# An own tile for the last step of a weight conversion, and other places for three steps of an attention pipeline among seven block products

## The chip, the cores and the metric

The kernel runs on one core of one Trainium2 chip. The metric is the device time of one execution in microseconds (us). A core has a tensor engine (PE), a vector engine (DVE), a scalar engine (ACT), GpSimd (POOL) and SyncE (SP), which issues nearly all transfers here. Each engine takes its instructions in the order of its own stream.

## The reference, cut to what matters

Attention without a mask whose softmax is taken over the features for q and over the sequence for k, then two feed-forward layers. The arrays of q, k and v are 8 x 8 x 576 x 64 in float32; the four weights are 512 x 2048 and 2048 x 512 in float64.

```python
q_s = softmax(q, axis=-1)                  # over the 64 features
k_s = softmax(k, axis=2)                   # over the 576 positions
kv  = einsum('bhsd,bhse->bhde', k_s, v)
x   = einsum('bhsd,bhde->bhse', q_s, kv)   # then 4608 tokens x 512
h = x @ w_in;  g = h / (1 + exp(-1.702 * h));  x = g @ w_out      # first layer
h = x @ w_in2; g = maximum(0.01 * h, h);       return g @ w_out2  # second layer
```

## The kernel before, in words

The 4608 tokens are nine chunks of 512, one for each batch entry and a rest. A float32 operand is held as two halves of a reduced format (hi and lo), and a product of two operands is three matmuls: hi·hi, lo·hi, hi·lo. The first matrix of a layer is applied to two chunks at a time, in blocks: seven products (ha, hb, hc in the names, six matmuls each) in place of eight, with sums of operands made beforehand and sums of results made on VectorE. One such group is a quad (`quad_step`); a pair of chunks has eight. The order of the products in a quad is a11, s2, s1, a12, s3, s4, and after a stretch of second-layer matmuls (acc) a22. Between the products stand numbered gaps, 0 to 9, lists of other work that is recorded there: gap 0 is ahead of the first product, gap 1 behind it, gap 2 behind the second, gap 4 behind the fourth. Pairs of layer 0 are named by their first chunk: (0,2) means layer 0, chunks 2 and 3. Eight quads serve the first matrix of the pair (`pair_first`) and the second matrix of its first chunk; then come sixteen steps for the second matrix of its second chunk (`pair_second`), called (0,3) for the pair (0,2).

While a pair is worked on, the attention of the next pair's chunks runs beside it, in units of one batch entry and two heads. `Units.tick()` starts a unit each quad and holds three at a time, in stages that it puts into the gaps:

- unit a: q and k are read. `k1` (L433) is the maximum of k over the rows of each partition, kmx.
- unit b: `k2` (L452) transposes kmx on TensorE into kma; `k3` (L457) reduces it to km on VectorE; `k4` (L462) transposes km back, spread over partitions, as kmb; `k5` (L468) subtracts it from the k tile kt, `k5b` (L476) takes the exponential on ScalarE. `q2` to `q4` are the same for q (qtp, L552). `k6` (L483) multiplies k and v to kvp; `k7` divides by the sums (krs, L495, L496) and writes the halves of kvt for two heads, L505 on ScalarE and L506 on VectorE in turn. Then `next_load` issues the loads for a unit to come, into the tiles that this unit has just freed.
- unit c: the x product (L591) multiplies q with kvt into pxt, and a ScalarE copy (L622) takes it to xr.

From pair (0,2) on, kma, kmb, qtp, kvp and pxt share one bank of PSUM, so each waits until the one before it has been read.

The weights of the second layer come as float64 and are converted in 32 steps while layer 0 runs, from (0,3) on (`conv_step`). `d0` loads a raw block (L94 or L100, raw). `d1` reads its low words (L110) and its high words (L113) on ScalarE into the two halves of a tile cv. `d2` works on them on VectorE: L117, L118, L127, and the last addition L131. `d3` stores the result (o<-cv, L210, or w<-cv, L213). The raw tile and cv come from one group of two buffers with the tag c4.

A framework with tiles sets the final order on each engine, the waits and the reuse of buffers when the program is built. The order in which the source records the instructions is where it starts from; it may move an instruction ahead of others that do not depend on it, unless `keep_in_program_order` holds it, as it does L110.

The code below is the kernel before, with the line numbers of the profile. In the changed kernel the lines behind 892 stand two lower.

Of the kernel before, what the change touches and what calls it, by code (L numbers as in the profile page):

```python
# [8 lines left out]
F32 = mybir.dt.float32  # L9
F32R = mybir.dt.float32r  # L10
AF = mybir.ActivationFunctionType
ALU = mybir.AluOpType
AX = mybir.AxisListType
U32 = mybir.dt.uint32
# [12 lines left out]
def tile_softmax_linear_attention_two_mlps(  # L27
# [16 lines left out]
    nc = tc.nc  # L44
    B, H, S, D = q.shape
    NT, DM = out.shape
    DFF = w_in1.shape[1]
    P = 128
    T = 512
# [31 lines left out]
    pool = dict(sb=sb, xa=xa)  # L81
# [22 lines left out]
    def words(raw):  # L104
        t = raw.bitcast(U32).rearrange("p (n two) -> p n two", two=2)
        return t[:, :, 0], t[:, :, 1]
# [8 lines left out]
    def convert2(w):  # L115
        wf = w.bitcast(F32)
        nc.vector.tensor_scalar(out=wf, in0=wf, scalar1=F64_LOW, scalar2=F64_HIGH, op0=ALU.max, op1=ALU.min)  # L117
        nc.vector.tensor_scalar(  # L118
            out=w, in0=w, scalar1=3, scalar2=0x3FFFFFF8, op0=ALU.logical_shift_left, op1=ALU.bitwise_and
        )  # L120

    def convert3(raws, low, w):
        n = 0
        for raw in raws:
            hw = words(raw)[1]
            o = slice(n, n + T)
            nc.vector.scalar_tensor_tensor(  # L127
                out=w[:, o], in0=hw, scalar=0xC0000000, in1=w[:, o], op0=ALU.bitwise_and, op1=ALU.bitwise_or
            )
            n += T  # L130
        nc.vector.tensor_tensor(out=w, in0=w, in1=low, op=ALU.add)  # L131

    WI = {}
    WO = {}
# [53 lines left out]
    part = {}  # L188
# [11 lines left out]
    def d2(n):  # L200
        r, t = part[n]
        convert2(t[:, 1, :])
        convert3([r], t[:, 0, :], t[:, 1, :])
        part[n] = t

    def d3(n):
        w = part.pop(n)[:, 1, :].bitcast(F32)
        f, i = divmod(n, 2)
        if i:
            nc.sync.dma_start(out=o32d[f // 2][:, f % 2, :], in_=w)  # L210
            return
        for b in range(2):
            nc.sync.dma_start(out=w4d[1][f // 2][:, BLOCK[f % 2, b], :], in_=w[:, 2 * P * b : 2 * P * (b + 1)])  # L213
# [251 lines left out]
    def k5(b, j):  # L465
        mv = kst.pop((b, j))[:, 0:P].rearrange("p (h d) -> p h d", h=2)
        km, *rest = kin[b, j]
        nc.vector.tensor_tensor(  # L468
            out=km, in0=km, in1=mv[:, :, None, :].to_broadcast([P, 2, km.shape[2], D]), op=ALU.subtract
        )  # L470
        for kr in rest:
            nc.vector.tensor_tensor(out=kr, in0=kr, in1=mv, op=ALU.subtract)

    def k5b(b, j):
        for t in kin[b, j]:
            nc.scalar.activation(t, t, AF.Exp)  # L476

    def k6(b, j):
        (km, *rest), (vm, vr) = kin.pop((b, j)), vin.pop((b, j))
        pk = bank("kvp", "h")  # L480
        for r in range(R + 1):
            for h in range(2):
                nc.tensor.matmul(  # L483
                    pk[h * D : (h + 1) * D, 0 : D + 1],
                    rest[0][:, h, :] if r == R and rest else km[:, h, r, :],
                    vm[:, h, r, :] if r < R else vr[:, h, :],
                    start=(r == 0),
                    stop=(r == R),
                )
        kst[b, j] = pk  # L490
# [283 lines left out]
    def new_g(side, f):  # L774
        if split:
            if f % 2 == 0:
                whole["g"] = pool["g"].tile([P, 2, T], F32, tag="a11", name="gs", bufs=4)
            return whole["g"][:, f % 2, :]
        if side == 1:
            return sb.tile([P, T], F32, tag="gf", name="gf", bufs=3)  # L780
        gb[f] = pool["gb"].tile([P, T], F32, tag="gb", name="gb", bufs=NF)
        return gb[f]
# [76 lines left out]
    def units_of(chunks):  # L859
        return [(c, j) for c in chunks for j in range(NP)]  # L860
# [12 lines left out]
    def empty():  # L873
        return [[] for _ in range(GAPS)]

    class Units:

        def __init__(self, chunks, done):  # L880
            self.todo = units_of(chunks)
            self.pipe = [None, None]
            self.done = done

        def tick(self):
            a = self.todo.pop(0) if self.todo else None
            b, c = self.pipe
            self.pipe = [a, b]
            out = empty()

            def at(i, fn, *u):
                out[i].append(lambda: fn(*u))

            if c:
                at(0, x_product, *c)
                at(0, self.done, *c)
            if b:
                at(1, q1b, *b, (1,))
                if b[0] < B:
                    at(2, k2, *b)  # L900
                    at(2, k3, *b)
                at(4, q2, *b)
                if b[0] < B:
                    at(4, k4, *b)
                    at(4, k5, *b)
                    at(5, k5b, *b)
                at(6, q3, *b)
                at(6, q4, *b)
                if b[0] < B:
                    at(8, k6, *b)  # L910
                    at(8, k7, *b)
                at(9, next_load)
            if a:
                at(8, q1, *a)
                if a[0] < B:
                    at(8, k1, *a)
                at(9, q1b, *a, (0,))
            return out
# [269 lines left out]
    def give(*names):  # L1188
        for name in names:
            pool[name].release()  # L1190
# [14 lines left out]
        k5=lambda j: k5(0, j), ke=lambda j: k5b(0, j), k6=lambda j: k6(0, j), k7=lambda j: k7(0, j),  # L1205
# [18 lines left out]
    units = Units([2, 3], x_raw)  # L1224
# [4 lines left out]
    for s in range(NF + LATER):  # L1229
        if own.busy:  # L1230
            gaps = own.tick()
        elif s % 2 == 0:
            half = units.tick() if units.busy and s + 1 < NF + LATER else empty()
            gaps = half[:5] + empty()[5:]
        else:
            gaps = empty()[:5] + half[5:]
# [9 lines left out]
        if s < NF:  # L1246
            h = g1(1, s)
            t = new_g(1, s)
# [32 lines left out]
        if s >= LATER:  # L1281
            h = g1(2, s - LATER)
            t = new_g(2, s - LATER)
# [121 lines left out]
    def chunks_of(layer, c):  # L1405
        return [c, c + 1] if c < LAST else [c]
# [41 lines left out]
    for i, (layer, c) in enumerate(order):  # L1448
        nxt = order[i + 1] if i + 1 < len(order) else None
        if split and c < LAST:  # L1450
            work = work_of(layer, c, nxt)
            fetched.clear()
            for n in range(NQ):
                gaps = empty()
                work(n, gaps)
                quad_apart(layer, n, gaps)
            pair_apart(c, second_steps(None, nxt), fetched)
        elif c < LAST:
            units = Units(chunks_of(*nxt), x_raw) if layer == 0 else None
            pair_first(layer, c, units, held, work_of(layer, c, nxt))  # L1460
            steps = second_steps(units, nxt)
            if layer == 0:
                for f in (0, 3, 6, 9, 11, 13):
                    spread(steps, conv_step(), f)
            else:
                spread(steps, sum_pieces(range(SUMS, NQ)), 0)
            held = pair_second(layer, c + 1, steps)
            if layer == 1:
                tail(*held)
                held = None  # L1470
                give("gb")
                sb.release()
                give("cv", "lo")
                take("left", "lo", "cv")
                take("right", "g")
                split = True
        elif layer == 0:
            assert not conv_step()
            sum_steps = sum_pieces(range(SUMS))
            places[:] = [1] * 4 + [0] * 6 + [1] * 4  # L1480
            pieces = build_pair(0)
            quad_pieces = first_quad(1, 0)[:1] + [lambda: None] + first_quad(1, 0)[1:]

            def work(f):
                if f + 3 < NF:
                    load_wi(layer, f + 3)
                load_wo(layer, f)
                if f == 0:
                    load_blocks(0)
                elif sum_steps:  # L1490
                    sum_steps.pop(0)()
                if f == 0:
                    load_x2(0)
                    load_x2(1)
                if 3 <= f < 12:
                    run(pieces[f - 3])
                if f >= 10:
                    quad_pieces.pop(0)()
                    if f >= 13:
                        quad_pieces.pop(0)()  # L1500
                if f >= 14:
                    load_o32(f - 14)

            held = single(layer, c, held, work)
            run(quad_pieces)
            for items in pieces[9:]:
                run(items)
        else:
            def work(f):
                if f + 3 < NF:  # L1510
                    load_wi(1, f + 3)
                load_wo(1, f)

            tail(*single(layer, c, None, work))
# [31 lines left out]
```

## Time and profile before

| | us |
|---|---|
| median of three runs | 1624.74 |
| the three runs | 1630.39, 1624.74, 1620.43 |
| the profiled execution | 1626.16 |
| its span, from the first instruction to the last | 1624.2 |
| TensorE busy in it | 1580.5 |
| mean granted clock of TensorE | 0.998 of full speed |

The profile comes from one execution. Busy time of TensorE is modelled: matmuls overlap, and a step of 512 columns takes 0.227 us where nothing waits. A row of the timeline says when an instruction starts, how long it takes, its engine, line, operation and operands, and in brackets how long its engine stood idle just before it and what ended that. A row of waits says who waited for whom, the sum in us, how often, and the longest. A landing time is counted from the issue of a transfer.

### The profile page before, as it was taken

The page shows a single profiled execution, that of the slowest core. Times are in us where ns is not written, and L with a number is a line of the kernel's source. Part 1 is how long each engine was busy: PE and PEld are TensorE (multiplying, and loading weights), DVE is VectorE, ACT ScalarE, POOL GpSimd, SP SyncE. Part 2 cuts the span into 40 slices and gives each one's busy share as a digit, 9 for nine tenths or more (in the row PEclk, how much of TensorE's full clock was granted, in tenths as well). Part 3 has the DMA queues.
Part 4 walks back from the last instruction along what each step waited for, and adds up shares of the span by engine and source line. Part 5 has one row for each costly group of instructions (what it writes and reads, how often), then busy time and mean ns, then how long its engine had stood idle before and what let it go on. Part 6 is the DMA issues. An engine that isn't in the chain of part 4 may idle for free.

```text
span 1624.2 us, 22216 instructions
## 1 busy us (share of the span) xinstructions
PE 1580.5 (97%) x7588; PEld 1275.0 (78%) x7588; DVE 1081.6 (67%) x1703; ACT 811.3 (50%) x1734; POOL 33.3 (2%) x167
## 2 busy tenths in 40 slices
PE   5999999999999999999999999999999999999998
PEld 3677777888777788788788888888888888888887
DVE  7899769887777767767544666644774486547411
ACT  7787755566545655435333545333453354334422
POOL 1000000000000000000000000000000000000000
PEclk9999999999999999999999999999999999999999
DMA  7788577888788887978996877986776777676763
GB/s 210 229 280 254 167 237 247 267 257 261 257 284 253 252 273 238 310 261 279 314 320 230 320 275 262 321 283 208 240 210 203 235 211 213 196 229 194 223 193 102
DMA packets 221904, 397.84 MB, mean 245 GB/s; under 512 B 57696, under 2 KB 138592, under 8 KB 221792
## 3 DMA queue, kind: packets, MB, share of 16 engines
q1 hardware_dynamic: 221792, 396.43, 76.2%
q8 instruction: 60, 0.98, 0.3%
q14 instruction: 52, 0.43, 0.1%
HBM read 306.18 MB, written 90.18 MB: 244 GB/s over the span
## 4 chain that ended last, share of the span: by engine, by line
PE 75%; DMA 6%; DVE 4%; issue 3%; ACT 2%; SPq 1%; POOL 0%; ACTq 0%; DVEq 0%; POOLq 0%
PE acc L824 22%; PE hb L767 12%; PE ha L767 8%; PE hc L767 8%; PE h L754 7%; PE ob L1091 6%; PE oa L1091 4%; PE oc L1091 4%; DMA o<-cv 2%; DMA w<-cv 2%; PE pxt L591 1%; PE otp L1039 1%; DMA qt<-in_q_dram 1%; DVE gl L87 1%; ACT cv L113 1%
## 5 line engine op out<-in xcount | busy, mean ns | idle before, releaser
L824 PE MATMUL acc<-gh,wo 128*128 128x512 f32 x1152 | 363.3, 396 | 2.9 <-ACT wo L84 1.8
L824 PEld LDWEIGHTS acc<-gh,wo 128*128 128x128 f32 x1152 | 211.3, 188 | 49.6 <-ACT wo L84 2.2
L824 PE MATMUL acc<-gl,wo 128*128 128x512 f32 x576 | 225.5, 392 | 0.0
L754 PE MATMUL h<-x,wi 128*128 128x512 f32 x768 | 190.5, 397 | 2.8 <-ACT wi L84 2.8
L754 PEld LDWEIGHTS h<-x,wi 128*128 128x128 f32 x768 | 143.5, 190 | 36.7 <-ACT wi L84 4.4
L767 PE MATMUL ha<-x,wa 128*128 128x512 f32 x624 | 162.3, 391 | 3.2 <-ACT p L940 2.7
L767 PEld LDWEIGHTS ha<-x,wa 128*128 128x128 f32 x624 | 115.8, 188 | 28.4 <-ACT p L940 3.9
L87 DVE TENSOR_TENSOR sl<-a,sh 128x1024 fp32r<-128x1024 f32 x84 | 102.7, 1223 | 49.3 <-ACT sh L84 49.0
L84 ACT CAST sh<-a 128x1024 fp32r<-128x1024 f32 x84 | 88.2, 1051 | 94.4 <-PE oc L1091 35.1
L824 PEld LDWEIGHTS acc<-gl,wo 128*128 128x128 f32 x576 | 108.1, 188 | 24.3 <-issue 0.6
L991 DVE TENSOR_TENSOR a<-hb,a 128x512 f32<-128x512 f32 x72 | 49.7, 691 | 92.8 <-PE hb L767 91.5
L767 PE MATMUL hb<-x,wc 128*128 128x512 f32 x384 | 97.4, 389 | 0.0
L528 ACT ACTIVATE qt<-qt,qmx 128x64 f32<-128x64 f32 x256 | 86.1, 339 | 13.2 <-DVE qmx L518 7.8
L1091 PE MATMUL ob<-sh,wo 128*128 128x512 f32 x288 | 91.6, 394 | 0.0
L767 PE MATMUL hb<-xb,wb 128*128 128x512 f32 x336 | 86.1, 390 | 0.0
L767 PEld LDWEIGHTS hb<-x,wc 128*128 128x128 f32 x384 | 72.1, 188 | 15.0
L84 ACT CAST gh<-gf 128x512 fp32r<-128x512 f32 x96 | 59.1, 616 | 43.7 <-DVE gf L792 37.1
L87 DVE TENSOR_TENSOR gl<-gb,gh 128x512 fp32r<-128x512 f32 x80 | 54.7, 687 | 39.0 <-ACT gh L84 38.7
L824 PE MATMUL acc<-wo,gh 128*128 128x512 f32 x256 | 78.9, 390 | 0.4 <-DMA wo<-wp 0.4
L84 ACT CAST gh<-gb 128x512 fp32r<-128x512 f32 x80 | 49.0, 618 | 57.6 <-PE acc L824 57.2
L87 DVE TENSOR_TENSOR gl<-gf,gh 128x512 fp32r<-128x512 f32 x96 | 66.0, 687 | 17.6 <-ACT gh L84 16.5
L788 ACT ACTIVATE a<-a 128x512 f32<-128x512 f32 x72 | 45.5, 632 | 64.2 <-DVE a L991 64.2
(191 smaller groups left out, 2899.3 us busy)
## 6 DMA issues: line engine op xcount, KB each, us to landing
wo<-wo SPq DMA_DIRECT2D x144, 512.0 KB, 4.7
wo<-wp SPq DMA_DIRECT2D x68, 512.0 KB, 3.6
wo<-wt SPq DMA_DIRECT2D x48, 512.0 KB, 3.6
wa<-wq SPq DMA_DIRECT2D x40, 512.0 KB, 4.4
wb<-wq SPq DMA_DIRECT2D x40, 512.0 KB, 4.5
wc<-wq SPq DMA_DIRECT2D x40, 512.0 KB, 4.7
raw<-in_moe_w_in_dram SPq DMA_DIRECT2D x32, 512.0 KB, 5.2
raw<-in_moe_w_out_dram SPq DMA_DIRECT2D x32, 512.0 KB, 4.9
```

The lines of the kernel that those rows point to most:

```text
L84: nc.scalar.copy(hi, src)
L87: nc.vector.tensor_tensor(out=lo, in0=src, in1=hi.bitcast(F32), op=ALU.subtract)
L113: nc.scalar.activation(w.bitcast(F32), hw.bitcast(F32), AF.Abs)
L528: nc.scalar.activation(t[:, h, r, :], t[:, h, r, :], AF.Exp, bias=mx[:, h, r : r + 1], accum_out=sm[:, h, r : r + 1],)
L591: nc.tensor.matmul(pv[:, :, a:e], w, m[:, :, a:e], start=(i == 0), stop=(i == 2))
L754: nc.tensor.matmul(h, WI[f][:, b, wh, o * P : (o + 1) * P], xs[f"a{side}{b + 1}"][xh][:, o, :], start=(i == 0), stop=(i == n - 1),)
L767: nc.tensor.matmul(h, w[:, wh, o * P : (o + 1) * P], xo[xh][:, o, :], start=(start and i == 0), stop=(i == 5), skip_group_check=not start,)
L788: nc.scalar.activation(t, h, AF.Prelu, alpha=0.01)
L824: nc.tensor.matmul(acc[d], lhsT, rhs, start=(f == 0 and i == 0), stop=(f == NF - 1 and i == 2))
L991: add = lambda out, h, t: nc.vector.tensor_tensor(out=out, in0=h, in1=t, op=ALU.add)
L1039: nc.tensor.transpose(pt[:, r * P : (r + 1) * P], t[:, r * P : (r + 1) * P], ident)
L1091: nc.tensor.matmul(banks[name][d], w[:, l, wh, sl], x[:, l, :], start=first_one, stop=(m == NQ // 2 - 1 and l == 1 and i == 2), skip_group ...
```

## The change

The change has two parts.

The conversion's addition L131 no longer writes into cv. It writes a tile of its own, co, with one buffer, and the store reads co. The tile cv is free when L131 has read it.

`Units` takes three numbers: the gap of the x product when the tick has a unit b, the gap of k2 and k3, and the gap of k4 and k5 (the exponential stands one gap behind). By default they are 0, 2 and 4 as before, but k2 to k5b are now recorded ahead of q1b and q2 of the same gap. The units that run beside pairs of layer 0 get 4, 1 and 2.

```diff
-    def convert3(raws, low, w):
+    def convert3(raws, low, w, to=None):
...
-        nc.vector.tensor_tensor(out=w, in0=w, in1=low, op=ALU.add)
+        nc.vector.tensor_tensor(out=w if to is None else to, in0=w, in1=low, op=ALU.add)
...
     def d2(n):
         r, t = part[n]
         convert2(t[:, 1, :])
-        convert3([r], t[:, 0, :], t[:, 1, :])
-        part[n] = t
+        part[n] = pool["cv"].tile([P, T], U32, tag="co", name="co", bufs=1)
+        convert3([r], t[:, 0, :], t[:, 1, :], part[n])
 
     def d3(n):
-        w = part.pop(n)[:, 1, :].bitcast(F32)
+        w = part.pop(n).bitcast(F32)
...
-        def __init__(self, chunks, done):
+        def __init__(self, chunks, done, gaps=(0, 2, 4)):
+            self.gaps = gaps
...
+            xg, mg, sg = self.gaps
             if c:
-                at(0, x_product, *c)
-                at(0, self.done, *c)
+                at(xg if b else 0, x_product, *c)
+                at(xg if b else 0, self.done, *c)
             if b:
+                if b[0] < B:
+                    at(mg, k2, *b)
+                    at(mg, k3, *b)
                 at(1, q1b, *b, (1,))
                 if b[0] < B:
-                    at(2, k2, *b)
-                    at(2, k3, *b)
+                    at(sg, k4, *b)
+                    at(sg, k5, *b)
+                    at(sg + 1, k5b, *b)
                 at(4, q2, *b)
-                if b[0] < B:
-                    at(4, k4, *b)
-                    at(4, k5, *b)
-                    at(5, k5b, *b)
...
-            units = Units(chunks_of(*nxt), x_raw) if layer == 0 else None
+            units = Units(chunks_of(*nxt), x_raw, (4, 1, 2)) if layer == 0 else None
```

Three places show what the built programs make of it. The first is TensorE in one quad of pair (0,4), from the end of the second-layer matmuls of the quad before. Before:

```order
L824 MATMUL acc_5001<-gl,wo 128x512
L767 MATMUL ha<-x,wa 128x512 x4
L591 MATMUL pxt<-qTh,kvt_142 128x4x96 x2
L591 MATMUL pxt<-qTl,kvt_142 128x4x96
L591 MATMUL pxt<-qTh,kvt_146 128x4x32 x2
L591 MATMUL pxt<-qTl,kvt_146 128x4x32
L767 MATMUL ha<-x,wa 128x512 x2
L767 MATMUL hb<-xb,wb 128x512 x6
L452 MATMUL kma<-ident,kmx 128x128
L767 MATMUL hc<-x,wb 128x512 x6
L767 MATMUL ha<-x,wa 128x512 x6
L462 MATMUL kmb<-ident,km 128x128
```

Changed:

```order
L824 MATMUL acc_5007<-gl,wo 128x512
L767 MATMUL ha<-x,wa 128x512 x6
L452 MATMUL kma<-ident,kmx 128x128
L767 MATMUL hb<-xb,wb 128x512 x6
L462 MATMUL kmb<-ident,km 128x128
L767 MATMUL hc<-x,wb 128x512 x6
L767 MATMUL ha<-x,wa 128x512 x6
L591 MATMUL pxt<-qTh,kvt_142 128x4x96 x2
L591 MATMUL pxt<-qTl,kvt_142 128x4x96
L591 MATMUL pxt<-qTh,kvt_146 128x4x32 x2
L591 MATMUL pxt<-qTl,kvt_146 128x4x32
```

The x product (pxt) stood inside the first product and stands behind the fourth; kma came up by one product, kmb by two, and one product now lies between them.

The second is VectorE in the same pair, from the end of one quad into the next (p, u and v are sums of products, krs and kvt belong to unit b of the quad that ends, kmx to the unit whose k tile is being loaded, km to the next quad's unit b). Before:

```order
L506 SCALAR_TENSOR_TENSOR kvt_142<-kvp,krs,kvt_142 64x64
L131 ISA cv_5432<-cv_5432 128x1024
L433 TENSOR_REDUCE kmx<-kt 128x128
L538 RECIPROCAL qsm<-qsm 128x8
L935 TENSOR_TENSOR u_5415<-hb,p_5399 128x512
L457 TENSOR_REDUCE km<-kma 128x1
L935 TENSOR_TENSOR v_5430<-hc,p_5399 128x512
L468 TENSOR_TENSOR kt<-kt,kmb 128x640
```

Changed:

```order
L506 SCALAR_TENSOR_TENSOR kvt_142<-kvp,krs,kvt_142 64x64 x2
L433 TENSOR_REDUCE kmx<-kt 128x128
L457 TENSOR_REDUCE km<-kma 128x1
L538 RECIPROCAL qsm<-qsm 128x8
L937 TENSOR_TENSOR u_5419<-hb,p_5399 128x512
L468 TENSOR_TENSOR kt<-kt,kmb 128x640
L937 TENSOR_TENSOR v_5433<-hc,p_5399 128x512
L131 ISA co<-cv_5436 128x1024
```

km moved from behind u to directly behind kmx, the subtract L468 ahead of v, and the conversion's addition L131 from ahead of kmx to behind v.

The third is ScalarE near the end of (0,3), where a unit's kvt is made. Before, then changed, in one piece each:

```order
L110 ACTIVATE cv_4538<-raw_4480 128x512
L84 CAST gh<-gb 128x512
L505 ACTIVATE kvt_145<-kvp,krs 64x64 x2
L622 COPY xr<-pxt 128x512
L84 CAST gh<-gb 128x512
L84 CAST x<-xr 128x1024
```

```order
L110 ACTIVATE cv_4538<-raw_4475 128x512
L84 CAST gh<-gb 128x512
L505 ACTIVATE kvt_145<-kvp,krs 64x64
L113 ACTIVATE cv_4653<-raw_4606 128x512
L505 ACTIVATE kvt_145<-kvp,krs 64x64
L84 CAST gh<-gb 128x512
L622 COPY xr<-pxt 128x512
```

L113 of the next conversion step, which reads a raw block, now stands between the two halves of kvt.

## Rows read from the trace of the kernel before

**Rows 1.** The page: busy time of engines; shares of the chain that ended last.

```profile
PE 1580.5 (97%) x7588; PEld 1275.0 (78%) x7588; DVE 1081.6 (67%) x1703; ACT 811.3 (50%) x1734; POOL 33.3 (2%) x167
PE 75%; DMA 6%; DVE 4%; issue 3%; ACT 2%; SPq 1%; POOL 0%; ACTq 0%; DVEq 0%; POOLq 0%
```

**Rows 2.** Stages: us, then busy us by engine, clock, DMA share, GB/s.

```profile
255.00:390.00 135.00, 134.32 (x737) 109.07 (x736) 118.75 (x219) 86.47 (x233) 5.61 (x35) 1.00 0.78 255
...
461.00:575.00 114.00, 108.62 (x596) 86.58 (x595) 86.88 (x165) 64.60 (x185) 5.05 (x30) 1.00 0.86 264
...
650.00:790.00 140.00, 137.57 (x608) 112.04 (x607) 99.55 (x157) 63.69 (x116) 0.23 (x1) 1.00 0.87 288
```

**Rows 3.** Waits of PE over the span: us, times, longest us.

```profile
PE pxt L591 <- DVE kvt L506: 5.3, 7, 2.2
PE kmb L462 <- DVE km L457: 3.4, 4, 1.6
```

**Rows 4.** The same waits of PE between 461 and 575 us.

```profile
PE pxt L591 <- DVE kvt L506: 4.8, 5, 2.2
PE kmb L462 <- DVE km L457: 0.5, 1, 0.5
```

**Rows 5.** Waits of ACT between 400 and 790 us, by the store.

```profile
ACT cv L110 <- DMA o<-cv: 17.2, 9, 3.0
ACT cv L110 <- DMA w<-cv: 16.9, 10, 4.8
```

**Rows 6.** Timeline of SP, ACT and PE where (0,4) begins.

```profile
435.76 0.33 SPq L100 DMA_DIRECT2D raw<-in_moe_w_out_dram  x1
...
440.54 0.68 ACT L110 ACTIVATE cv<-raw 128x512 uint32<-128x512 uint32 x1 [2.38 <-DMA w<-cv]
...
444.94 1.42 PE L767 MATMUL ha<-x,wa 128*128 128x512 f32 x5 [1.71 <-ACT p L940]
```

**Rows 7.** Landing times of the loads issued at 435.76, 337.24, 510.30, 408.40.

```profile
DMA to landing us min/median/max: 3.7/3.7/3.7
...
DMA to landing us min/median/max: 4.2/4.2/4.2
...
DMA to landing us min/median/max: 5.2/5.2/5.2
...
DMA to landing us min/median/max: 5.0/5.0/5.0
```

**Rows 8.** Timeline of PE in (0,4): the longest wait of the x product.

```profile
495.64 0.59 PE L591 MATMUL pxt<-qTh,kvt 128*128 128x384 f32 x2 [2.18 <-DVE kvt L506]
```

**Rows 9.** Timeline of one quad's transposes in (0,2), DVE, PE and SP.

```profile
335.92 0.80 PE L483 MATMUL kvp<-vt,kt 128*64 128x65 f32 x20
...
337.24 0.63 SPq L359 DMA_DIRECT2D kt<-in_k_dram  x1
...
341.58 1.31 DVE L433 TENSOR_REDUCE kmx<-kt 128x128 f32<-128x640 f32 x1 [0.94 <-DMA kt<-in_k_dram]
...
342.98 0.27 PE L452 MATMUL kma<-ident,kmx 128*128 128x128 f32 x1
...
343.86 0.28 DVE L457 TENSOR_REDUCE km<-kma 128x1 f32<-128x128 f32 x1
```

**Rows 10.** The same for a quad of (0,4) with a late k load.

```profile
515.63 1.31 DVE L433 TENSOR_REDUCE kmx<-kt 128x128 f32<-128x640 f32 x1 [1.26 <-DMA kt<-in_k_dram]
...
516.74 0.27 PE L452 MATMUL kma<-ident,kmx 128*128 128x128 f32 x1
```

**Rows 11.** Timeline of (0,3): a raw load, the second L505, the x product.

```profile
408.40 0.33 SPq L100 DMA_DIRECT2D raw<-in_moe_w_out_dram  x1
...
412.16 0.31 ACT L505 ACTIVATE kvt<-kvp,krs 64x64 fp32r<-64x64 f32 x1 [0.34 <-DVE kvt L506]
...
412.94 0.53 PE L591 MATMUL pxt<-qTh,kvt 128*128 128x320 f32 x2
```

**Rows 12.** Waits of DVE between 250 and 790 us, for the k load.

```profile
DVE kmx L433 <- DMA kt<-in_k_dram: 8.5, 7, 4.2
```

## The prediction, before the change was run

> **What bounds the kernel now.** The page was read first. TensorE is busy 97% of the span and holds 75% of the chain that ended last [rows 1], so a change here can win at most what TensorE stands still for, unless the amount of its work changes; it does not (the same instructions, moved). Second, the busy time by stage [rows 2]: TensorE idles 0.7 us in the steps that go with chunk pair (0,2), 5.4 us in those of (0,4), 2.4 us in (0,6). Past 790 us the instruction order is the same in both programs. Third, TensorE's waits: over the span 5.3 us for the x product's operand kvt and 3.4 us for km, the operand of the transpose kmb [rows 3]; 4.8 and 0.5 us of these lie in the steps of (0,4) [rows 4]. Fourth, ScalarE's waits in the weight conversion [rows 5]: 19 waits of L110, 34.1 us in all, that end when a store out of the conversion's tile has landed. They are the largest waits that the change touches, but ScalarE's and not TensorE's. So two questions decide: which of the waits of rows 3 and 4 go, and what the two transposes, drawn together, wait for instead.
>
> **The change part by part.** Durations come from the profiled execution, 1626.16 us, 1.4 above the median of 1624.74; I sum on the first and subtract the 1.4. Plus is slower.
>
> *The own tile.* The step's add (L131) writes co, so the buffer of cv is free at the add's end and not when the store has landed. What is next is the raw load that the same ScalarE instruction reads. In the step shown, L110 starts at 440.54 after 2.38 us of waiting for the store [rows 6]; the raw load issued at 435.76 needed 3.7 us [rows 7], so it was there at 439.5, and 1.1 us is won. Over the steps I found 0.6 to 1.9 us apiece, some 18 us for ScalarE. TensorE sees that only where it waits behind ScalarE: at 444.94 it waited 1.71 us for p, a ScalarE copy that stood behind L110, L113 and eight exponentials [rows 6]. I credit 0.7 us for this; the bounds are 0 (the load is as late) and 2.5 (that wait and one more like it go). A later add would wait for the previous store of co, which is a whole step old: nothing.
>
> *The x product moves behind the fourth product.* It is 0.7 us of TensorE in either place. Before, the order put it in the middle of the first product, about 3 us behind kvp, whose result must first pass through VectorE, ScalarE and VectorE to become kvt; with conversion instructions between them VectorE finished late and TensorE waited 2.18 us [rows 8]. After, three products (some 4 us) more stand between. The 4.8 us [rows 4] go, and with 0.5 of kmb and small change I take **-5.9 us** in (0,4); bounds -4.8 and -6.5. The transpose bank is single (kma, kmb, the x product, the transposes of q and kvp share it), so the x product now needs kt's subtract to have read kmb, two products or 2.7 us ahead of it; the subtract reads as many elements as kmx, which takes 1.31 us [rows 9], and this bounds it. It fits, unless VectorE is late with more than one instruction ahead of it: 0.
>
> *The transposes move up.* Here is the price. Before, kma stood behind the second product and kmb behind the fourth, so km (0.28 us on VectorE [rows 9]) had 2.7 us to be made. Now one product, 1.36 us, lies between. That alone would do. But in VectorE's new order km stands behind kmx, the reduction of the *next* unit's k tile (1.31 us), in 11 of the steps of (0,2) and (0,4), and kmx waits for a load that goes out only when kvp has released the tile. In the step of (0,2) shown [rows 9] kvp starts at 335.92, the load is issued at 337.24 and needs 4.2 us [rows 7]; kmx starts when it lands, at 341.58. Now kmb can start no sooner than 341.58 + 1.31 + 0.28, about 343.1 with overlaps. TensorE would reach it at the old place of kma, 342.98, less the 0.7 of the x product that no longer stands ahead, plus 0.1 for kma: 342.4. A wait of 0.7 us. By the same sum the five steps of (0,2) give 0, 0.4, 0.7, 0.3 and 0.5: **+1.9 us**, bounds 0 and 3. In (0,4) the dearest is the load that needs 5.2 us [rows 7]: kmx at 515.63, kmb possible at 517.2; TensorE there at 516.74 less the old wait of 0.4 and the 0.6: 1.5 us [rows 10]. The six steps give 0.9, 0.6, 1.5, 0, 1.3 and 0: **+4.3 us**, bounds 1 and 6.
>
> The Trainium skill, "DMA: Bandwidth & Descriptors", section "Anatomy of one DMA — SWDGE (gpsimd) path", fits one transfer as 2.0 us plus its bytes over 436 GB/s; by it the 256 KB of kt would need 2.6 us (estimate), kmx would start well before kma, and the +6.2 us of this part would be 0, the first rival below. The fit is for transfers issued by GpSimd, and the trace does not bear it out for these: the rows show 4.2 and 5.2 us [rows 7], and the DMA engines were over three quarters busy there [rows 2], so I keep the rows.
>
> *The order on ScalarE in pairs (0,3) and (0,5).* The new order puts L113 of the next conversion step between the two halves of kvt (L505) of one unit. L113 waits for a raw load. At (0,3) that load goes out at 408.40 and needs 5.0 us [rows 7, 11], so it lands at 413.4; the second L505 was at 412.16 and the x product that needs it at 412.94. Now: 413.4 + 0.7 for L113 (taken as long as L110 [rows 6]), 0.31 for L505 and as much for L506 on VectorE, so the x product at about 414.8: **+1.9 us**. (0,5) has the same piece with a load of 4.9 us: **+1.8**. Bounds for both together 0 (the load leaves earlier by 2 us) and 5.
>
> *Stage before 255 us.* Here the gaps are the default ones, and only the order changes: kt's subtract and exponential are recorded ahead of q2. VectorE is the fuller engine, and earlier exponentials bring kvp earlier; against it kmb stands one product-matmul behind kma at places. Of the 3.4 us of kmb waits 2.9 are before 461 us [rows 3, 4]. I take **-0.5**, bounds -3.5 and +3. (0,6) and later: 0, bounds of 1 either way, since only the conversion's waits change.
>
> Sum: -0.7 - 5.9 + 1.9 + 4.3 + 1.9 + 1.8 - 0.5 = **+2.8 us**. 1626.16 + 2.8 = 1629.0, less 1.4: **1627.5 us**. One per cent, 16 us, is about what a measurement of this kernel tells from no change; the three runs shown already differ by 10.
>
> **The rivals.** *The waits just go (faster).* For it: the loads' landing times vary with what runs beside them; VectorE might be done with kmx before kma, as in one step of (0,2). Then the 6.2 us of the transposes and the 3.7 us of L113 are about 0, and -7 to -9 remain: 1616 to 1618. Against it: 7 of the kmx in this stretch already wait for the landing of their load, 8.5 us in all [rows 12]. To come under 1608.5, 16 us would have to go, and the stages of rows 2 have 8.5 us of idle TensorE together; so "faster by over 1%" gets little.
>
> *The k load becomes the bound (slower).* One mechanism: kmb stands behind km, km behind kmx, kmx behind a load that is only issued when the unit before releases its tile. It decides from the point where kmx starts more than about 4.1 us after kvp's last matmul (340.8 for the step of rows 9). Each microsecond by which the load lands later goes straight to TensorE in all 11 steps, and a stalled TensorE has nothing behind the transpose that it may take up. With 1 us more a step than in rows 9 and 10, the sum is +2.8 + 11: 1638; with 1.3 us more the 1% is passed, 1641. For it: the load at 510 needed 5.2 us where that at 337 needed 4.2 [rows 7]; own-tile conversion starts its raw loads earlier and they go through the same queues. Against it: landings would have to be later than almost all that the trace has.
>
> *Nothing to speak of.* The conversion's wait for the store turns into one for the raw load, and the stalls at the x product change place with those at kmb: 0 within 2, 1623 to 1627. By kind this is my forecast with the terms rounded down.
>
> **How the numbers follow.** Chances: the forecast, swapped stalls with a small loss (+1 to +7), 0.45; nothing to speak of, 0.25; the waits just go, 0.17; the load becomes the bound, 0.13, of which less than half passes 1%. The likeliest time is 1627.5. Adding the bounds that work together on the good side gives -8 to -10, on the bad side +12; the range runs from 1616 to 1637. Faster by over 1%: 0.04. Slower by over 1%: 0.06. Within 1%: 0.90.
>
> **What would show it.** In the profile after: no wait of L110 or L113 for a store, but waits of 0.5 to 3 us for the raw load; no wait of the x product for kvt in the quads of (0,4); new waits of kmb for km, up to about 1.5 us, in steps where kmx starts at its load's landing; one wait of about 2 us for kvt near 414 and one near 608; past 790 us the same intervals as before. I am wrong if kmb does not wait (then kmx was done in time, and the time is near 1617), if waits of 2 us and more stand at every kmb (near 1640), or if the stage before 255 us moves by more than 4 us.

## The result, and the profile after

The changed kernel took 1645.96 us in the median (1638.1 to 1647.89, 4 runs) against 1624.76 us before: a ratio of 1.0112, 95% interval 1.0079 to 1.0145. (The two medians by themselves make 1.0130.) So it is slower by 18 to 21 us. The forecast was 1627.5 us in a range of 1616 to 1637, with 0.06 on slower by over 1%. Measured again on another chip beside the experiments below, the ratio was 1.0103 (1.0087 to 1.0119). The profiled execution of the changed kernel took 1647.9 us, its span is 1646.0 us.

Where did the 22 us between the two spans come in? The same matmul can be found in both traces; the table has when TensorE starts it, and in its last row when the last matmul ends.

```
first matmul of                before     changed   later by   added in
pair (0,2)                     254.44      256.64      2.2     first stage      +2.2
last quad of (0,2)             374.42      378.32      3.9     (0,2)            +1.7
pair (0,4)                     438.98      446.87      7.9     (0,3)            +4.0
last quad of (0,4)             567.30      580.69     13.4     (0,4)            +5.5
pair (0,6)                     632.98      649.67     16.7     (0,5)            +3.3
last quad of (0,6)             745.00      763.51     18.5     (0,6)            +1.8
end of the last matmul        1620.10     1640.93     20.8     rest             +2.3
```

So 14.5 us come in from (0,2) to (0,5), where attention runs beside the pairs. In a second profile of the changed kernel, taken on another chip, these four stages add 1.3, 2.1, 5.1 and 5.7 us, 14.2 in all: a single stage differs by about 2 us between executions, the sum hardly. What does TensorE wait for there? TensorE's waits in the changed kernel between 255 and 830 us (us, times, longest):

```profile
PE kmb L462 <- DVE km L457: 9.3, 8, 2.0
PE pxt L591 <- DVE kvt L506: 3.6, 2, 2.1
PE kma L452 <- DVE kvt L506: 3.4, 5, 1.4
```

Against [rows 4], where the x product waited 4.8 us for kvt and kmb 0.5 us for km: the x product's waits in the quads of (0,4) are gone, two of 2.1 and 1.5 us in (0,3) and (0,5) have come, kmb waits 9.3 us, and kma, which waited for nothing there, waits for kvt. (In the second profile these three are 7.8, 3.5 and 2.4 us.)

The waits are not all. From 90 us to the last matmul the granted clock of TensorE is 1.00 throughout in the kernel before. In the changed kernel it falls to 0.50, the lower of its two levels (1.2 and 2.4 GHz), twice: just behind the wait of 2.05 us for kvt that ends at 419.64, and just behind one of 2.00 us for km that ends at 564.26. Rows of two stretches, in the form of [rows 2]:

```profile
421.03:424.44 3.41, 3.41 (x10) 2.64 (x9) 3.41 (x4) 1.89 (x3) 0.00 (x0) 0.50 0.57 168
564.39:567.80 3.41, 3.41 (x9) 2.69 (x9) 1.70 (x3) 1.30 (x2) 0.00 (x0) 0.50 0.08 18
```

TensorE is busy all through both, so each costs an estimated 1.7 us, half its length. From (0,2) to (0,5) TensorE's idle time goes from 7.8 us to 17.1. With the estimated 3.4 us of the clock that is 12.7 of the 14.5 us.

The waits of DVE and ACT in the quads of (0,4) and, for ACT, from 400 to 810 us:

```profile
DVE cv L117 <- ACT cv L113: 8.9, 6, 2.2
DVE kmx L433 <- DMA kt<-in_k_dram: 7.5, 5, 2.2
```

```profile
ACT cv L113 <- DMA raw<-in_moe_w_in_dram: 16.0, 7, 3.7
ACT cv L110 <- DMA raw<-in_moe_w_in_dram: 11.5, 4, 4.8
ACT cv L110 <- DMA raw<-in_moe_w_out_dram: 11.2, 7, 3.9
ACT cv L113 <- DMA raw<-in_moe_w_out_dram: 8.6, 7, 2.1
```

In the quads of (0,4) the kernel before had less of both waits of VectorE:

```profile
DVE cv L117 <- ACT cv L113: 6.1, 3, 2.5
DVE kmx L433 <- DMA kt<-in_k_dram: 1.7, 2, 1.3
```

In the changed kernel no wait for a store is left, but ScalarE waits 47.3 us in all for raw loads, as much as it waited for stores before (34.1 us of L110 [rows 5] and 13.9 of L113). Half of it, 24.6 us, now stands at L113.

One quad of (0,4) shows how the waits hang together. First ScalarE and VectorE, at the end of the quad before:

```profile
534.86 0.66 ACT L113 ACTIVATE cv<-raw 128x512 f32<-128x512 f32 x1 [1.47 <-DMA raw<-in_moe_w_in_dram]
...
535.55 0.43 DVE L117 TENSOR_SCALAR cv<-cv 128x512 f32<-128x512 f32 x1 [1.31 <-ACT cv L113]
...
538.42 0.15 DVE L495 TENSOR_SCALAR krs<-kvp 128x1 f32<-128x1 f32 x1
...
540.46 0.29 DVE L506 SCALAR_TENSOR_TENSOR kvt<-kvp,krs,kvt 64x64 fp32r<-64x64 f32 x1 [0.38 <-ACT kvt L505]
542.63 1.23 DVE L433 TENSOR_REDUCE kmx<-kt 128x128 f32<-128x640 f32 x1 [1.89 <-DMA kt<-in_k_dram]
543.89 0.29 DVE L457 TENSOR_REDUCE km<-kma 128x1 f32<-128x128 f32 x1
```

and TensorE, in the same stretch:

```profile
535.80 0.52 PE L483 MATMUL kvp<-vt,kt 128*64 128x65 f32 x12
...
540.89 0.30 PE L452 MATMUL kma<-ident,kmx 128*128 128x128 f32 x1 [0.25 <-DVE kvt L506]
...
544.24 0.32 PE L462 MATMUL kmb<-ident,km 128*128 128x128 f32 x1 [1.66 <-DVE km L457]
```

L113 waits for its raw load; L117 on VectorE waits for L113, and with it all that VectorE has behind it: krs starts 2.3 us after the start of kvp's last matmul. In the six quads of (0,4) it starts 2.1 to 3.0 us behind that; before, four of the six had 1.0 to 1.7. kvt is therefore done at 540.75 and kma, which needs the bank that kvt was read from, can go only then. Behind kvt VectorE takes kmx, which waits until 542.63 for the k load, then km, and kmb waits for that. Two late loads stand in one chain that ends on TensorE twice in a quad.

In (0,3), the place of [rows 11], the predicted piece is there:

```profile
418.05 0.66 ACT L113 ACTIVATE cv<-raw 128x512 f32<-128x512 f32 x1 [2.10 <-DMA raw<-in_moe_w_out_dram]
418.74 0.31 ACT L505 ACTIVATE kvt<-kvp,krs 64x64 fp32r<-64x64 f32 x1
...
419.64 0.54 PE L591 MATMUL pxt<-qTh,kvt 128*128 128x320 f32 x2 [2.05 <-DVE kvt L506]
```

and in (0,2) the predicted wait for the k load:

```profile
326.61 1.24 DVE L433 TENSOR_REDUCE kmx<-kt 128x128 f32<-128x640 f32 x1 [2.14 <-DMA kt<-in_k_dram]
327.88 0.29 DVE L457 TENSOR_REDUCE km<-kma 128x1 f32<-128x128 f32 x1
...
328.22 0.32 PE L462 MATMUL kmb<-ident,km 128*128 128x128 f32 x1 [1.44 <-DVE km L457]
```

### The profile page after: what moved, and what is told of

Same layout as the page of the kernel before. It is cut to its first block, busy times and chain, and to the rows that moved or that the text cites. A ratio compares the mean times of both kernels' runs of the same rounds, so it can differ in the third digit from the quotient of the medians.

```text
span 1646.0 us, 22186 instructions
## 1 busy us (share of the span) xinstructions
PE 1589.1 (97%) x7588; PEld 1277.4 (78%) x7588; DVE 1085.4 (66%) x1703; ACT 812.4 (49%) x1734; POOL 33.8 (2%) x167
## 4 chain that ended last, share of the span: by engine, by line
PE 71%; issue 9%; DMA 8%; DVE 5%; ACT 2%; POOL 0%; SPq 0%; ACTq 0%; DVEq 0%; POOLq 0%
PE acc L824 21%; PE hb L767 11%; PE hc L767 8%; PE ha L767 7%; PE h L754 7%; PE ob L1093 6%; PE oa L1093 4%; PE oc L1093 4%; DMA kt<-in_k_dram 2%; DMA raw<-in_moe_w_in_dram 2%; DMA raw<-in_moe_w_out_dram 2%; DMA wo<-wo 1%; DVE cv L127 1%; PE pxt L591 1%; PE otp L1041 1%
## 5 line engine op out<-in xcount | busy, mean ns | idle before, releaser
L84 ACT CAST sh<-a 128x1024 fp32r<-128x1024 f32 x84 | 88.2, 1050 | 94.4 <-PE oc L1093 35.1
L767 PE MATMUL hc<-x,wb 128*128 128x512 f32 x288 | 76.0, 399 | 0.0
```

Of the source, the lines that this page charges most:

```text
L84: nc.scalar.copy(hi, src)
L767: nc.tensor.matmul(h, w[:, wh, o * P : (o + 1) * P], xo[xh][:, o, :], start=(start and i == 0), stop=(i == 5), skip_group_check=not start,)
```

## The experiments

The theory after the result (A): two causes, and they feed each other. km stands behind kmx, which waits for the k load; and the own tile lets the framework put L113 further ahead, so that ScalarE and then VectorE stand waiting for a raw load just where kvt is made. The rivals (B to I) put the loss on one of the two parts, on the chip, or on VectorE's lateness as such. All ratios are to the kernel before, run beside on the same chip, with 95% intervals; its median there was 1628.9 to 1629.5 us.

### The two parts apart

The own tile alone leaves the gaps and the recording order as they were.

> The kernel before with the own tile co alone, steps at their old gaps. Theory A (two causes add up: the conversion's L113 now waits for its raw load ahead of other ScalarE work, and km waits behind kmx): the first cause alone, about 2 us each in (0,3) and (0,5) and 2 to 4 in (0,4), so 1629 to 1634. Rival B (the new places of the transposes do all of it): 1622 to 1628, and no new wait on TensorE.

Measured: 1.0011 (0.9997 to 1.0026), 1631.9 us. That lies in theory A's range in microseconds, but the kernel before took 1629.4 on this chip, and the interval holds 1: no loss is shown. Both ranges were made from 1624.8 us; as ratios to that, A's is 1.003 to 1.006 and is missed, and the time does not speak against B. The two pieces of L113 between the halves of kvt are in this kernel as well, and TensorE's waits between 255 and 830 us are

```profile
PE pxt L591 <- DVE kvt L506: 5.1, 5, 1.7
PE ha L767 <- ACT p L940: 4.9, 4, 1.7
```

so alone the own tile moves waits (that for p grew from 2.7 us to 4.9) and costs little. ScalarE's waits for raw loads come to 35.1 us in its trace, 13 less than the waits for stores before, and TensorE has nothing from it. The gaps and the recording order without the own tile:

> The changed kernel without the own tile: new gaps and recording order, cv stored as before. Theory A: kmb waits of 9 us in (0,2) and (0,4), less some 5 us of x product waits that go, plus 2 in the first stage: 1629 to 1635. Rival B (the gaps do all of it): 1643 to 1648. Rival C (the own tile does all of it): 1622 to 1628.

Measured: 1.0056 (1.0037 to 1.0074), 1639.4 us against 1629.4, 9 to 10 us slower. In microseconds that is above theory A's range; as a ratio to 1624.8 us the range was 1.003 to 1.006, and the measured one lies in it. Its waits:

```profile
PE kmb L462 <- DVE km L457: 9.0, 8, 2.4
PE ha L767 <- ACT p L942: 2.7, 2, 1.7
PE kma L452 <- DVE kvt L506: 2.0, 3, 0.8
```

The kmb waits are all there without the own tile, and the x product's waits for kvt are gone as A had it. What A did not count are the waits of kma and the clock, which falls in this trace too: to 0.50 for 3.4 us twice in (0,4), behind waits of kmb of 2.40 and 2.19 us. And L113 is late here without the own tile: in (0,4) it waits 10.3 us for stores out of cv, where in the changed kernel it waits 11.8 us for raw loads, VectorE waits 12.5 us for it in both, and (0,4), counted as in the table, takes 134.4 us here, 133.8 in the changed kernel and 128.3 before. B and C fall: neither part does it all. And the parts do not add up: 1.0011 and 1.0056 make 1.0067, while the whole has

> The changed kernel itself, beside the others on one chip. Theory A' (own tile and gaps cost more together, +18 to +20, than the +2 and +9 that they cost alone): ratio 1.009 to 1.013 to the kernel before. Rival F (the two add up and the rest was the chip of the first comparison): ratio 1.005 to 1.008.

1.0103 (1.0087 to 1.0119), 1645.9 us. Rival F falls; some 6 us, by the three intervals between 1 and 11, come only from the two together. In the profiles they do not stand in (0,4), which the new gaps alone lengthen as much. They show in (0,5): 65.7 us before, 65.9 with the own tile, 66.9 with the new gaps, 69.0 and 71.4 in the two profiles with both. There the x product and kma wait 2.4 us for kvt in either of these two profiles, and in the longer one the clock falls once more.

The recording order alone (k2 to k5b ahead of q1b and q2, default gaps for all):

```diff
-            units = Units(chunks_of(*nxt), x_raw, (4, 1, 2)) if layer == 0 else None
+            units = Units(chunks_of(*nxt), x_raw) if layer == 0 else None
```

> The kernel before with the new recording order alone (k2 to k5b ahead of q1b and q2), default gaps everywhere, no own tile. Theory A: the first stage's 2 us and nothing else, ratio 1.000 to 1.002. Rival: the recording order carries the loss of the new gaps, ratio 1.004 to 1.008.

Measured: 1.0008 (0.9997 to 1.0019). The loss is not the recording order's.

### Taking one cause out of the changed kernel

kmx is recorded at gap 8, but the built program had it directly behind kvt, ahead of the next quad's km (the second place in the part on the change). Recorded at gap 6 and held there, it comes after the k5 of its quad, when the load has had some 10 us more:

```diff
     def k1(b, j, pin=False):
...
+        if pin:
+            tc.keep_in_program_order(i)
...
-                    at(8, k1, *a)
+                    if self.late:
+                        at(6, k1, *a, True)
+                    else:
+                        at(8, k1, *a)
```

> The changed kernel with kmx (L433) of layer 0's later units recorded at gap 6 and held there in program order, so that km no longer stands behind it and the k load has 10 us more. Theory A: the kmb waits of 9.4 us past 255 us fall to under 2, and 1636 to 1640 results. Rival D (km is late because VectorE as a whole is late, by the conversion's wait, and kma waits for the bank until kvt is made): km starts as late as before, 1643 to 1648.

Measured: 1.0031 (1.0015 to 1.0046), 1635.1 us, 11 us under the changed kernel and just below A's range.

```profile
PE pxt L593 <- DVE kvt L508: 3.3, 2, 1.8
PE kma L454 <- DVE kvt L508: 1.7, 2, 1.3
PE kmb L464 <- DVE km L459: 1.5, 2, 1.1
```

The kmb waits fell from 9.3 us to 1.5 as A expected, and D falls. The x product's two waits in (0,3) and (0,5) stay: they are the other cause's. Between 90 us and the last matmul the clock does not fall, here or in the next two kernels. (Holding one instruction lets the framework move others. Against the changed kernel, the order on TensorE is the same here, but some 110 of VectorE's 1703 instructions stand elsewhere; with L113 held it is some 190, and 5 of TensorE's. So neither run moves one instruction alone.) Holding L113 in program order as L110 is held takes that one out:

```diff
-        nc.scalar.activation(w.bitcast(F32), hw.bitcast(F32), AF.Abs)
+        i = nc.scalar.activation(w.bitcast(F32), hw.bitcast(F32), AF.Abs)
+        if pin:
+            tc.keep_in_program_order(i)
```

> The changed kernel with L113 of the second layer's conversion held in program order too, as L110 already is. Theory A: L113 no longer stands between the halves of kvt nor ahead of gb and kvt, so the two x product waits of 2.1 and 1.5 us in (0,3) and (0,5) and the kma waits for kvt (3.4 us) go: 1638 to 1642. Rival E (the raw load lands late wherever L113 stands, and what waits behind it only changes its name): 1644 to 1648.

Measured: 1.0016 (1.0003 to 1.0029), 1632.1 us, 14 us under the changed kernel, where A expected 4 to 8. E falls; A had the sign and was short in size. It counted some 7 us of waits for kvt; it did not count that the kmb waits shrink with them, from 9.3 us (7.8 in the second profile) to 6.1, nor that the clock no longer falls, an estimated 3.4 us.

```profile
PE kmb L464 <- DVE km L459: 6.1, 6, 2.6
```

is the one large wait that is left between 255 and 830 us: neither the x product nor kma waits for kvt. ScalarE still waits for the raw loads, 30.5 us in that kernel:

```profile
ACT cv L110 <- DMA raw<-in_moe_w_in_dram: 16.5, 5, 6.0
ACT cv L110 <- DMA raw<-in_moe_w_out_dram: 14.0, 7, 4.6
```

It waits at L110, in the middle of a quad, and no longer just ahead of gb, krs and kvt. So the sum of ScalarE's waits alone does not decide: it was 48.0 us before and 47.3 in the changed kernel. Where they stand does.

Both held:

> The changed kernel with L113 held in program order and kmx held at gap 6: both suspects taken away, the new gaps and the own tile kept. Theory A: the kmb waits that L113's pin alone left past 255 us, some 6 us, go as well: 3 to 8 us under the kernel with L113 pinned alone, ratio to the kernel before 0.997 to 1.001. Rival G (with one mended, TensorE waits for the next late thing, p or kvt): within 2 us of L113 pinned alone, ratio 1.000 to 1.003.

Measured: 0.9984 (0.9974 to 0.9995), 1626.4 us. It is 5.7 us under L113 held alone (5.2 by the ratios, as the two ran on different chips), as A expected; G falls. With the own tile and the new gaps both in it, this kernel is 0.16% faster than the one before.

Four kernels now show that the two causes feed each other. Counted from both held, the ratio grows by 0.0032 when kmx alone is let go, by 0.0047 when L113 alone is, and by 0.0119 with both: 0.0040, some 6.5 us, more than the sum (by the intervals, 2 to 11). The length of (0,4) in the profiles says the same: 122.7 us with both held, 125.3 and 124.7 with one let go, 133.8 with both.

VectorE and TensorE in one quad of its (0,4), whose lines stand two lower at kmx and four lower from kma on:

```profile
521.86 1.28 DVE L435 TENSOR_REDUCE kmx<-kt 128x128 f32<-128x640 f32 x1
...
523.70 0.80 PE L487 MATMUL kvp<-vt,kt 128*64 128x65 f32 x20
...
526.07 0.15 DVE L499 TENSOR_SCALAR krs<-kvp 128x1 f32<-128x1 f32 x1
...
527.57 0.29 DVE L510 SCALAR_TENSOR_TENSOR kvt<-kvp,krs,kvt 64x64 fp32r<-64x64 f32 x1 [0.38 <-ACT kvt L509]
...
528.66 0.27 PE L456 MATMUL kma<-ident,kmx 128*128 128x128 f32 x1
528.97 0.29 DVE L461 TENSOR_REDUCE km<-kma 128x1 f32<-128x128 f32 x1 [1.11 <-PE kma L456]
```

kmx is done before kvp with no wait for its load, kma finds kvt read, and VectorE stands ready for km. The Trainium skill ("DMA: Bandwidth & Descriptors", "Rules for kernel authors") has it that a transfer is issued early and its semaphore waited for late. The trace agrees: the k load is issued at the same place in both kernels, and only the wait was moved, from 11.0 us in 8 waits of kmx past 255 us in the changed kernel to none in the quads of (0,4) here.

### What the new gaps are worth

Own tile and both pins at the old gaps:

> The kernel before with own tile, L113 held in program order and kmx held at gap 6, at the old gaps. In the old order kmb had two products of room, so kmx ahead of km cost TensorE nothing: theory A expects the time of the kernel before, ratio 0.997 to 1.001, and the x product's waits for kvt still there (4 to 6 us). Rival H (a late kmx helps by itself, since VectorE waits 8.5 us for the k load in the old order too): ratio under 0.996.

Measured: 1.0004 (0.9993 to 1.0016). H falls; the x product's waits for kvt are still there, 4.2 us, as A expected. At the old gaps the own tile and both pins together gain nothing. That a late kmx costs nothing there is seen with the own tile alone: in (0,4) kmx waits 7.7 us for its load, and kmb not at all. New gaps and kmx held, without the own tile:

> The kernel with the new gaps and no own tile, with kmx held at gap 6. Theory A: the kmb waits past 255 us (9 us there) fall to under 2 and the ratio from 1.0056 to 0.998 to 1.002. Rival D (km is late with or without kmx ahead of it): 1.004 to 1.006.

Measured: 0.9988 (0.9975 to 1.0001), against 1.0056 with kmx where the framework put it. The kmb waits past 255 us are 1.5 us and the clock does not fall there. A holds and D falls: the 9 us of the new gaps were kmx's place. The transposes at gaps 1 and 2 with the x product at its old gap 0:

```diff
-            units = Units(chunks_of(*nxt), x_raw, (4, 1, 2)) if layer == 0 else None
+            units = Units(chunks_of(*nxt), x_raw, (0, 1, 2)) if layer == 0 else None
```

> The kernel before (no own tile) with the transposes at gaps 1 and 2 and the x product at its old gap 0. Theory A (the 9 us that the new gaps cost alone are the transposes' waits for km behind kmx, and the x product's move gave some of that back): kmb waits as in the kernel with the new gaps, x product waits as before, ratio 1.005 to 1.009. Rival I (the x product at gap 4 is what costs, by its wait for kt's subtract and the copy behind it): ratio 1.000 to 1.003.

Measured: 1.0053 (1.0033 to 1.0073). The ratio is A's and the reason is not:

```profile
PE pxt L591 <- DVE kvt L506: 6.8, 6, 1.9
PE kma L452 <- ACT xr L622: 2.3, 4, 0.8
PE kmb L462 <- DVE km L457: 1.0, 3, 0.4
```

Here the x product stands ahead of kma and takes the wait for kvt, kma waits for the copy that empties the bank, and kmb, later by both, finds km nearly done. My expectation of its kmb waits failed. The one bank passes the wait on to whichever of its users stands first behind kvp. These waits are 4.8 us more than in the kernel before. The clock falls twice to 0.50 for 3.4 us here too, behind waits of 1.82 us for p and 1.95 us for kvt, an estimated 3.4 us; together that is about the 8.6 us measured. Rival I falls. This order with kmx held was not run, so what makes kvt late in it stays open.

Last, both pins with the first stage in its old recording order:

> The kernel with both pins (own tile, new gaps, L113 and kmx held), with the first stage's units in the old recording order, so that only the steps from 255 us on are changed. Theory A: the first stage's 1 to 2 us come back, ratio 0.996 to 0.998. Rival: they were the spread of one profile, ratio as with both pins, 0.998 to 0.999.

Measured: 0.9963 (0.9949 to 0.9977), 1624.5 us against 1629.5: 5 us faster than the kernel before, as A expected; the whole interval lies just under the rival's range. It is the fastest here, though its interval and that of both pins just overlap. In its trace the first matmul of (0,2) comes at 254.3 us, as before, and that of (0,6) at 627.5 against 633.0.

## Why the prediction was wrong

**What bounds the kernel** was read rightly: TensorE's work is the same, and what moved were its waits, most of them in the stages named, and with them its clock.

**The own tile** (-0.7): alone +0.1%, within the spread. The step that failed is the credit for ScalarE's waits. Alone it shortened them by 13 us (I had 18), but not on TensorE's path, and in the changed kernel not at all: 47.3 us after 48.0. The one wait for p that I wanted to shorten is gone, but others came: waits for p make 1.5 us in the changed kernel after 2.7, and 4.9 with the own tile alone. That the freed L113 would stand ahead of gb and kvt in (0,4) was in the order; I costed it only where it stood between the two halves of kvt, in (0,3) and (0,5).

**The x product** (-5.9 in (0,4)): this is the step that failed most, by 4.5 us. I wrote that kma, the x product and kvp share one bank and followed that for the x product alone. With the x product out of the way, kma is the first behind kvp to need the bank, one product into the next quad, and what makes kvt must have read it: 3.4 us came back as waits of kma for kvt, 2.5 of them in (0,4). I also took kvt's time for granted where VectorE was to wait for L113 right ahead of it. -5.9 became about -1.4 in waits that TensorE shows.

**The transposes** (+6.2, in eleven steps): the mechanism was right, one load to one place. In size the waits of kmb came to 9.3 us between 255 and 830 us, 8.8 more than before. In (0,2) I had +1.9 and 1.7 came in. In (0,4) I had 4.3 and the rows have 7.6 us in 6 waits: kmx started later than I took it, since kvt ahead of it was late and its loads landed 4.6 to 5.8 us after their issue in (0,4), where it had been 2.5 to 5.2. One reading was wrong without harm to the sum: the 4.2 and 5.2 us of [rows 7] belong to L359, a load of 32 KB for the same tile, issued 0.44 us behind the one of 256 KB (L358). It lands last, by 0.2 us, and so ends the wait of kmx. The 256 KB took 4.5 and 5.4 us there, so my answer to the fit of 2.6 us stands.

**L113 between the halves of kvt** (+1.9 and +1.8): waits of 2.05 and 1.5 us. Right in mechanism and size. The table adds 4.0 and 3.3 us in (0,3) and (0,5). The rest of (0,3) is the clock, an estimated 1.7 us; in (0,5) it is waits of TensorE for kvt at kma (0.9 us) and for a copy of results (0.7 us).

**The clock** stood in no term. Its two falls cost an estimated 3.4 us past 255 us, one behind the wait for kvt that I had forecast for (0,3), the other behind a wait of kmb.

**The first stage** (-0.5): +2.2 in the trace, inside its bounds, on the other side. In the profiles of the eight kernels with the new recording order there, (0,2) starts 1.1 to 4.1 us later than before; in the three with the old one it starts 0.6 earlier to 1.0 later. In every profile with the new order TensorE waits 1.80 us for a weight block near 80 us and has the clock at 0.50 for 3.4 us behind it; in none with the old order does that wait stand there. (0,6) and what follows (0): +4.1 in this profile, of which the experiments do not tell what is the spread of single loads: waits for second-layer weights of 2.3 us where 1.0 stood before.

**The rivals.** The one on the slow side, the k load as the bound, was the nearest, with 0.13, and its 11 steps are the largest single part. It was not enough: it reached 1641, and what it lacked is the second late event in the same chain, L113. I had added the two up as separate terms, each with its own bounds. They do not add: kvt's lateness pushes kmx, kmx pushes km, and in the four kernels with one, both or neither held the two together cost some 6.5 us more than each by itself. (That is not the 6 us between the two parts of the change: without the own tile L113 is late too, waiting for a store.) The bad side of the range, +12, was a sum of separate bounds and therefore too short.

**What the miss is made of.** The forecast was +2.8 us, and the last matmul ends 20.8 us later. Of the 18 us between, the x product is 4.5, (0,6) and what follows 4.1, the clock 3.4, the first stage 2.7 and the transposes 2.6, waits and estimates of one profile. No one of these alone would have taken the time out of the range.

That neither part is bad by itself is what the experiments add. With kmx and L113 held in place, the same two parts give 0.9984, and with the old start 0.9963.

## What to carry to other kernels

When a step on a shared bank is moved away, ask who is now the first user behind the writer; the wait goes to that one. When the order is made by a scheduler, look in the built order for instructions that wait for a load and have been moved ahead of work on which the bound engine waits, on every engine of that chain; holding two of them in place turned a loss of 1.0% into a gain of 0.2%. Late events in one chain are to be costed along the chain, not as separate terms. And look at the granted clock behind every long wait of TensorE: here the wait cost its own length and, at times, 1.7 us more.

## What the runs showed of the hardware that was not expected

The k loads of 256 KB (L358) landed 2.8 to 6.1 us after their issue between 255 and 600 us of the changed kernel. Their median was 4.1 us before, and 4.6 and 4.4 us in two profiles of the changed kernel. An order that leaves such a load less than 6 us can't be costed with one figure.

TensorE's clock fell to 0.50 after waits shorter than its longest waits at full clock. Four profiles have two falls each between 255 and 1600 us: both of the changed kernel, that of the new gaps and that of the transposes at gaps 1 and 2. All four are of kernels slower by 0.5% or more. Each fall comes 0.1 to 1.7 us after TensorE has resumed from a wait of 1.7 to 2.4 us, and lasts 3.4 us. The other nine profiles have none there, though the kernel before waited 2.18 us [rows 8] and the one with L113 held 2.62 us. So the length of the wait alone does not tell whether the clock falls.
